# MLP layer 1 and q with the weights as the moving operand in four column groups; w1 in one transfer

## Chip, cores, metric

One core of one Trainium2 chip. The metric is the device time of one execution in microseconds (us), the median of several; all times are of the fast state unless said otherwise. The profile of a kernel is one execution, read as its page, its chain of waits, its timeline, and the records of its DMA packets. PE is the tensor engine (PEld its weight loads), DVE the vector engine, ACT the scalar engine, POOL is GpSimd, and SP issues the big loads.

## The reference

One token, D = 576. Attention over the last 4096 of 32768 cached positions (32 query heads, 16 key heads of 128), an MLP of width 4608, and a gate that mixes the two:

```python
x = A_x
g = _sigmoid((x * gate_w).sum(-1, keepdims=True))
# attention: q = x @ wq; scores over the last W = 4096 keys; softmax; p @ v; then @ wo
a = _A_ref(x, A_k_cache, A_v_cache, A_wq, A_wo)
# MLP: gelu(x @ w1 + b1) @ w2 + b2
b = _B_ref(x, B_w1, B_b1, B_w2, B_b2)
return g * a + (1 - g) * b
```

All operands are bfloat16. The data that must be read are 16.8 MB of keys, as much of values, and 20 MB of weights: 53.6 MB for one token.

## The kernel before

The small rows go through the ACT queue, everything big through the SP queue, in the order in which it is needed. `w1_t` and `wq_t` share their buffers ("B", "A") with later k tiles, so the third k tile (g = 2) can be asked for only when layer 1 is done with w1, and the fourth when q is done with wq.

```python
    rows = kt_pool.tile([2, 8192], BF16, name="rows", tag="kt")
    x_row = rows[0:1, 0:D]
    gw_row = rows[0:1, D : 2 * D]
    b2_row = rows[0:1, 2 * D : 3 * D]
    b1_t = rows[0:2, 3 * D : 3 * D + FH]
    xdup = rows[0:1, 3 * D + FH : 5 * D + FH]
    junk_row = rows[0:1, 5 * D + FH : 6 * D + FH]
    nc.scalar.dma_start(out=x_row, in_=A_x.rearrange("a b d -> (a b) d"))
    nc.scalar.dma_start(out=gw_row, in_=gate_w.rearrange("(o n) -> o n", o=1))
    nc.scalar.dma_start(out=b2_row, in_=B_b2.rearrange("(o n) -> o n", o=1))
    nc.scalar.dma_start(out=b1_t, in_=B_b1.rearrange("(h n) -> h n", h=2))


    w1_t = big.tile([P, NI, FH], BF16, name="w1_t", tag="B")
    w1_src = B_w1.rearrange("d (h n) -> (d h) n", h=2).rearrange("(p i) n -> p i n", i=NI)
    for i0, i1 in ((0, 4), (4, NI)):
        nc.sync.dma_start(out=w1_t[:, i0:i1, :], in_=w1_src[:, i0:i1, :])
    wq_t = big.tile([P, NI, QH], BF16, name="wq_t", tag="A")
    wq_src = A_wq.rearrange("d (h n) -> (d h) n", h=2).rearrange("(p i) n -> p i n", i=NI)
    for i0, i1 in ((0, NI),):
        nc.sync.dma_start(out=wq_t[:, i0:i1, :], in_=wq_src[:, i0:i1, :])
# ... (masks and constants on GpSimd cut)
```

Layer 1 and q use the weights as the stationary operand (`lhsT`), 128 columns at a time, and stream two columns of x through them. That gives each result its place on 128 partitions at once, for 162 + 144 weight loads:

```python
    h_ps = ps_m.tile([P, NF], FP32, name="h_ps", tag="m")
    for j in range(NJ):
        nc.tensor.matmul(
            h_ps[:, j:NF:NJ],
            lhsT=b1_t[:, j:FH:NJ],
            rhs=ident[0:2, 0:2],
            start=(j == 0),
            stop=False,
            skip_group_check=True,
        )
    QZ = 24
    qz_flat = const.tile([P, QZ + 4 * NG * P + 96], BF16, name="qz_flat")
    nc.gpsimd.memset(qz_flat[:].bitcast(FP32), 0.0)
    for i in range(NI):
        for j in range(NJ):
            nc.tensor.matmul(
                h_ps[:, j:NF:NJ],
                lhsT=w1_t[:, i, j:FH:NJ],
                rhs=x2[:, i, :],
                start=False,
                stop=(i == NI - 1 and j == NJ - 1),
                skip_group_check=True,
            )
    hacc = const.tile([P, NF], FP32, name="hacc")
    nc.vector.tensor_copy(out=hacc[:], in_=h_ps[:])
# ... (gelu on DVE and ACT cut)
    q_ps = ps_m.tile([P, Hq], FP32, name="q_ps", tag="m")
    for i in range(NI):
        for j in range(Hq // 2):
            nc.tensor.matmul(
                q_ps[:, j : Hq : Hq // 2],
                lhsT=wq_t[:, i, j * Dh : (j + 1) * Dh],
                rhs=x2[:, i, :],
                start=(i == 0 and j == 0),
                stop=(i == NI - 1 and j == Hq // 2 - 1),
                skip_group_check=True,
            )
    q_b = const.tile([P, Hq], BF16, name="q_b")
    nc.scalar.copy(out=q_b[:], in_=q_ps[:])
# ... (q is spread into qz_flat by four products and four ACT casts)
```

The loads of the caches, by tag, and the transpose that frees them:

```python
    def load(name, tag, cache, g):
        tile_ = big.tile([P, NCK, Dh], BF16, name=name, tag=tag)
        src = cache[0, HB * g : HB * g + HB, Sk - W : Sk, :].rearrange(
            "b (k c) d -> k b (c d)", k=NKP
        )
        nc.sync.dma_start(out=tile_[:].rearrange("p c d -> p (c d)"), in_=src)
        return tile_

    k_t, s_ps, kt = [None] * NG, [None] * NG, {}

    def transpose(g, f):
        if f == 0:
            k_t[g] = load("k_t", "CDBA"[g], A_k_cache, g)
        kt[g, f] = kt_pool.tile([P, SL * Dh], BF16, name="kt", tag="kt")
        keys = k_t[g][:, f * SL : (f + 1) * SL, :]
        queue(
            "dve",
            lambda: nc.vector.transpose(
                out=kt[g, f][:].bitcast(FP32),
                in_=keys.rearrange("p c d -> p (c d)").bitcast(FP32),
            ),
        )
```

The rest (scores, softmax, values, output projection and layer 2, summed in `y_ps`) is the same in both kernels. After the k tiles the order of the loads is two v tiles, w2's first half, the third v tile, a few tail rows of wo (on four of the 16 DMA engines), the fourth v tile, wo in two transfers, and w2's second half in three; the last 16 products follow the last of these.

Of the kernel before, what the change touches and what calls it, by code (L numbers as in the profile page):

```python
# [9 lines left out]
FP32 = mybir.dt.float32  # L10
BF16 = mybir.dt.bfloat16
I32 = mybir.dt.int32
ACT = mybir.ActivationFunctionType
ALU = mybir.AluOpType
# [4 lines left out]
def kernel(  # L19
# [15 lines left out]
    nc = tc.nc  # L35

    P = 128
    D = 576
    Hq, Hkv, Dh = 32, 16, 128
# [7 lines left out]
    FH = F // 2  # L47
    NJ = FH // P
    NF = 2 * NJ
    NI = 2 * D // P  # L50
    QH = Hq * Dh // 2
    DH = D // 2
# [153 lines left out]
    const = ctx.enter_context(tc.tile_pool(name="const", bufs=1))  # L206
    big = ctx.enter_context(tc.tile_pool(name="big", bufs=1, side="right"))
    kt_pool = ctx.enter_context(tc.tile_pool(name="kt_pool", bufs=2, side="right"))
    ps_s = ctx.enter_context(tc.tile_pool(name="ps_s", bufs=2, space=bass.MemoryType.PSUM))
    ps_y = ctx.enter_context(tc.tile_pool(name="ps_y", bufs=1, space=bass.MemoryType.PSUM))  # L210
    ps_m = ctx.enter_context(tc.tile_pool(name="ps_m", bufs=2, space=bass.MemoryType.PSUM))


    rows = kt_pool.tile([2, 8192], BF16, name="rows", tag="kt")
    x_row = rows[0:1, 0:D]
    gw_row = rows[0:1, D : 2 * D]
    b2_row = rows[0:1, 2 * D : 3 * D]
    b1_t = rows[0:2, 3 * D : 3 * D + FH]
    xdup = rows[0:1, 3 * D + FH : 5 * D + FH]
    junk_row = rows[0:1, 5 * D + FH : 6 * D + FH]  # L220
# [5 lines left out]

    w1_t = big.tile([P, NI, FH], BF16, name="w1_t", tag="B")
    w1_src = B_w1.rearrange("d (h n) -> (d h) n", h=2).rearrange("(p i) n -> p i n", i=NI)
    for i0, i1 in ((0, 4), (4, NI)):
        nc.sync.dma_start(out=w1_t[:, i0:i1, :], in_=w1_src[:, i0:i1, :])  # L230
    wq_t = big.tile([P, NI, QH], BF16, name="wq_t", tag="A")
    wq_src = A_wq.rearrange("d (h n) -> (d h) n", h=2).rearrange("(p i) n -> p i n", i=NI)
# [10 lines left out]
    for base, pattern, keep in (  # L243
# [13 lines left out]
        out=is0[:], in0=low[:], scalar1=0.0, scalar2=None, op0=ALU.is_equal  # L257
    )
    alt = is0[:, 0 : 2 * NI].rearrange("p (i t) -> p i t", t=2)
    ones = const.tile([P, P], FP32, name="ones")  # L260
    nc.gpsimd.memset(ones[:], 1.0)
    ident = const.tile([P, P], BF16, name="ident")
    make_identity(nc, ident[:])
    RW = 31
    NZ = 512 + 5 * RW + 1 + 64
    zeros = const.tile([P, NZ + 4 * D], BF16, name="zeros")
    nc.gpsimd.memset(zeros[:].bitcast(FP32), 0.0)
    perm = zeros[:, 0:512].rearrange("p (j b l) -> p j b l", j=4, b=4)
    at31 = zeros[:, 512 : 512 + 5 * RW].rearrange("p (a r) -> p a r", a=5)
# [3 lines left out]
        out=perm,  # L273
        in_=perm,
        pattern=[[-64, 2], [-1, 2], [0, 4], [-2, 32]],
        compare_op=ALU.not_equal,
        fill=1.0,
        base=0,
        channel_multiplier=1,
    )  # L280
    nc.gpsimd.affine_select(
        out=at31,
        in_=at31,
        pattern=[[-RW, 5], [-1, RW]],
        compare_op=ALU.not_equal,
        fill=1.0,
        base=0,
        channel_multiplier=1,
# [3 lines left out]
        out=hi5[:],  # L292
        in_=ones[:, 0:5],
        pattern=[[-RW, 5]],
        compare_op=ALU.is_ge,
        fill=0.0,
        base=0,
        channel_multiplier=1,
    )
    nc.gpsimd.affine_select(  # L300
        out=hi5[:],
        in_=hi5[:],
        pattern=[[RW, 5]],
        compare_op=ALU.is_ge,
        fill=0.0,
        base=RW - 1,
        channel_multiplier=-1,
# [4 lines left out]
        out=hi16[:], in0=is0[:, c0 : c0 + 16], scalar1=-SCALE, scalar2=None, op0=ALU.mult  # L312
# [5 lines left out]
        out=row_of[:],  # L318
        in_=row_of[:],
        pattern=[[0, 16], [-1, HB], [0, 2]],  # L320
        compare_op=ALU.not_equal,
        fill=1.0,
        base=0,
        channel_multiplier=1,
# [4 lines left out]
        out=foreign[:],  # L329
        in_=foreign[:],  # L330
        pattern=[[0, P], [-1, HB]],
        compare_op=ALU.not_equal,
        fill=0.0,
        base=0,
        channel_multiplier=1,
# [4 lines left out]
        out=xdup.rearrange("p (d t) -> p d t", t=2),  # L340
        in_=x_row.rearrange("p (d o) -> p d o", o=1).to_broadcast([1, D, 2]),
    )
    xs_ps = ps_m.tile([P, NI, 1], FP32, name="xs_ps", tag="m")
    for i in range(NI):
        nc.tensor.matmul(  # L345
            xs_ps[:, i, :],
            lhsT=xdup[:, i : 2 * D : NI],
            rhs=one_b[0:1, 0:1],
            start=(i == 0),
            stop=(i == NI - 1),  # L350
            skip_group_check=True,
        )
    x2 = const.tile([P, NI, 2], BF16, name="x2")
    nc.vector.tensor_tensor(
        out=x2[:], in0=xs_ps[:].to_broadcast([P, NI, 2]), in1=alt, op=ALU.mult
    )


# [2 lines left out]
        out=junk_row,  # L361
        in0=x_row,
        in1=gw_row,
        scale=1.0,
        scalar=0.0,
        op0=ALU.mult,
        op1=ALU.add,
# [9 lines left out]
    omg = const.tile([P, 1], FP32, name="omg")  # L377
    nc.vector.tensor_scalar(
        out=omg[:], in0=g_t[:], scalar1=-1.0, scalar2=1.0, op0=ALU.mult, op1=ALU.add
    )  # L380
    b2g = const.tile([1, D], FP32, name="b2g")
    nc.vector.tensor_scalar(
        out=b2g[:], in0=b2_row, scalar1=omg[0:1, 0:1], scalar2=None, op0=ALU.mult
    )
    gh = const.tile([P, 1, 5], FP32, name="gh")
# [1 line left out]
        out=gh[:, 0, :], in0=hi5[:], scalar1=g_t[:, 0:1], scalar2=None, op0=ALU.mult  # L387
# [18 lines left out]
    y_add(ones[0:1, 0:1], b2g[0:1, :], start=True)  # L406


    h_ps = ps_m.tile([P, NF], FP32, name="h_ps", tag="m")
    for j in range(NJ):  # L410
        nc.tensor.matmul(
            h_ps[:, j:NF:NJ],
            lhsT=b1_t[:, j:FH:NJ],
            rhs=ident[0:2, 0:2],
            start=(j == 0),
            stop=False,
            skip_group_check=True,
        )
    QZ = 24
    qz_flat = const.tile([P, QZ + 4 * NG * P + 96], BF16, name="qz_flat")  # L420
    nc.gpsimd.memset(qz_flat[:].bitcast(FP32), 0.0)
    for i in range(NI):
        for j in range(NJ):
            nc.tensor.matmul(  # L424
                h_ps[:, j:NF:NJ],
                lhsT=w1_t[:, i, j:FH:NJ],
                rhs=x2[:, i, :],
                start=False,
                stop=(i == NI - 1 and j == NJ - 1),
                skip_group_check=True,  # L430
            )
    hacc = const.tile([P, NF], FP32, name="hacc")
    nc.vector.tensor_copy(out=hacc[:], in_=h_ps[:])  # L433
    z2 = const.tile([P, NF], FP32, name="z2")
    nc.vector.tensor_tensor(out=z2[:], in0=hacc[:], in1=hacc[:], op=ALU.mult)
    C0 = 0.7978845608028654
    poly = const.tile([P, NF], FP32, name="poly")
    nc.vector.tensor_scalar(
        out=poly[:],
        in0=z2[:],  # L440
        scalar1=2.0 * C0 * 0.044715,
        scalar2=2.0 * C0,
        op0=ALU.mult,
        op1=ALU.add,
    )
    u_t = const.tile([P, NF], FP32, name="u_t")
    nc.vector.tensor_tensor(out=u_t[:], in0=poly[:], in1=hacc[:], op=ALU.mult)
    e_h = const.tile([P, NF], FP32, name="e_h")
    nc.scalar.activation(out=e_h[:], in_=u_t[:], func=ACT.Exp, scale=-1.0)
    nc.vector.tensor_scalar(out=e_h[:], in0=e_h[:], scalar1=1.0, scalar2=None, op0=ALU.add)  # L450
# [1 line left out]
    nc.vector.reciprocal(out=r_t[:], in_=e_h[:])  # L452
    gt = const.tile([P, NF], BF16, name="gt")
    nc.vector.scalar_tensor_tensor(
        out=gt[:], in0=hacc[:], scalar=omg[:, 0:1], in1=r_t[:], op0=ALU.mult, op1=ALU.mult
    )


    q_ps = ps_m.tile([P, Hq], FP32, name="q_ps", tag="m")
    for i in range(NI):  # L460
        for j in range(Hq // 2):
            nc.tensor.matmul(  # L462
                q_ps[:, j : Hq : Hq // 2],
                lhsT=wq_t[:, i, j * Dh : (j + 1) * Dh],
                rhs=x2[:, i, :],
                start=(i == 0 and j == 0),
                stop=(i == NI - 1 and j == Hq // 2 - 1),
                skip_group_check=True,
            )
    q_b = const.tile([P, Hq], BF16, name="q_b")  # L470
    nc.scalar.copy(out=q_b[:], in_=q_ps[:])
    qj_ps = ps_m.tile([P, 4, NG, 8], FP32, name="qj_ps", tag="m")
    for j in range(4):
        nc.tensor.matmul(
# [293 lines left out]
```

## Time and profile before

| | before |
|---|---|
| time | 131.68 us (131.63 to 131.78) |
| span of the profiled run | 130.1 us |
| load queue, share of 16 engines | 96.5% (125.5 us) |
| layer 1 ends / q ready / first k tile transposed from | 24.2 / 32.7 / 36.7 us |
| last load lands / end | 127.2 / 130.1 us |

The lines behind this table stand in the prediction below. A line of the timeline reads: start, duration, engine, source line, operation, output <- inputs, shapes, count; the bracket tells how long the engine sat idle before it and what ended that. Source lines differ between the kernels (L531 before is L569 after); go by the tiles. Two lines of the timeline of the kernel before are needed later, for the small rows of x and of b1:

```profile
6.09 0.75 DVE L339 COPY rows<-rows 1x1152 bf16<-1x1152 bf16 x1 [6.09 <-DMA rows<-in_A_x_dram]
...
10.49 1.28 PE L411 MATMUL h_ps<-ident,rows 2*128 2x2 bf16 x18 [1.36 <-DMA rows<-in_B_b_dram]
```

### The profile page before, as it was taken

To read this page: it belongs to the slowest core of one execution; us is meant where nothing else is said; L and a number is where in the kernel's file an instruction comes from. 1 tells how busy PE (TensorE), PEld (TensorE's weight loads), DVE (VectorE), ACT (ScalarE), POOL (GpSimd) and SP (SyncE) were. 2 spreads that over 40 slices of the span, in tenths; PEclk is the share of its full clock that TensorE was granted. 3 is DMA by queue.
4 is the path that set the end of the run, shared out by engine and by line. 5 is a ranking of instruction groups with operands and counts; after the bars stand their busy time and mean duration, and the time that the engine had idled before them with its cause. 6 is when DMAs were issued, how large, how long until landed. Compare 5 with 4: busy or idle time off the path is not lost.

```text
span 130.1 us, 2403 instructions
## 1 busy us (share of the span) xinstructions
PE 79.7 (61%) x1148; PEld 45.6 (35%) x1077; DVE 52.3 (40%) x48; ACT 8.3 (6%) x18; POOL 9.2 (7%) x26
## 2 busy tenths in 40 slices
PE   0037999476003998939918994995300830899573
PEld 0037679375000121201211120595300830855441
DVE  0153000400079959999999995614000020010001
ACT  2000000003000000030003003011000000000001
POOL 7039700000000000000000000000000000000000
PEclk9999999999999999999997799985555555559999
DMA  6999999799899999999899899899899899999980
GB/s 232 427 431 432 476 424 476 344 484 448 373 458 453 403 433 463 393 433 484 373 433 484 383 423 484 357 432 505 368 433 489 363 438 415 442 401 427 413 363 33
DMA packets 2508, 53.75 MB, mean 413 GB/s; under 512 B 286, under 2 KB 290, under 8 KB 580
## 3 DMA queue, kind: packets, MB, share of 16 engines
q1 hardware_dynamic: 2490, 53.61, 96.5%
q8 instruction: 8, 0.13, 0.4%
q10 hardware_dynamic: 10, 0.01, 0.0%
HBM read 53.62 MB, written 0.00 MB: 412 GB/s over the span
## 4 chain that ended last, share of the span: by engine, by line
DMA 52%; DVE 24%; PE 14%; issue 6%; SPq 2%
DMA k_t<-in_A_k_cache_dram 27%; DMA w_t<-in_B_w_dram 25%; DVE kt L531 19%; PE s_ps L553 7%; PE o_ps L640 5%; DVE m L569 3%; DVE pt L602 2%; PE y_ps L396 1%; SPq L684 1%; DVE mr L572 1%; SPq L691 0%; DVE out_row L736 0%; SPq L234 0%; SPq L230 0%; PE mt_ps L578 0%
## 5 line engine op out<-in xcount | busy, mean ns | idle before, releaser
L553 PE MATMUL s_ps<-kt,qz_flat 128*128 128x512 bf16 x128 | 32.9, 414 | 17.2 <-DVE kt L531 10.4
L531 DVE STREAM_TRANSPOSE kt<-k_t 128x4096 f32<-128x4096 f32 x8 | 35.3, 4433 | 12.2 <-DMA k_t<-in_A_k_cache_dram 10.5
L640 PE MATMUL o_ps<-pt,v_t 128*128 128x8 bf16 x512 | 14.2, 168 | 16.6 <-DMA v_t<-in_A_v_cache_dram 14.7
L553 PEld LDWEIGHTS <-qz_flat 128*128 128x128 bf16 x64 | 6.9, 107 | 40.6 <-issue 40.4
L640 PEld LDWEIGHTS <-v_t 128*128 128x128 bf16 x512 | 14.0, 102 | 17.3 <-DMA v_t<-in_A_v_cache_dram 14.9
L424 PEld LDWEIGHTS <-w_t 128*128 128x128 bf16 x162 | 10.3, 167 | 1.8 <-issue 1.8
L424 PE MATMUL h_ps<-x,w_t 128*128 128x2 bf16 x162 | 10.5, 202 | 0.0
L590 ACT ACTIVATE p_t<-s_ps,negm 128x1024 bf16<-128x1024 f32 x4 | 4.5, 1114 | 50.9 <-DVE negm L586 50.9
L396 PE MATMUL y_ps<-w_t,gt 128*1 128x288 bf16 x72 | 6.3, 329 | 1.2 <-DMA w_t<-in_B_w_dram 1.2
L670 DVE RECIPROCAL rg<-mt_ps 128x32 f32<-128x32 f32 x1 | 0.4, 358 | 15.6 <-PE mt_ps L665 15.6
L602 DVE STREAM_TRANSPOSE pt<-p_t 128x1024 bf16<-128x1024 bf16 x4 | 4.9, 1225 | 2.7 <-ACT p_t L590 2.7
L462 PE MATMUL q_ps<-x,wq_t 128*128 128x2 bf16 x144 | 4.0, 166 | 2.9 <-DMA wq_t<-in_A_wq_dram 2.9
L569 DVE TENSOR_REDUCE m<-s_ps 128x1 f32<-128x1024 f32 x4 | 4.8, 1196 | 1.1 <-PE s_ps L553 1.1
L396 PE MATMUL y_ps<-wo_t,ov 128*1 128x288 bf16 x62 | 4.3, 285 | 1.4 <-DMA wo_t<-in_A_wo_dram 1.4
L736 DVE CAST out_row<-y_ps 1x288 bf16<-1x288 f32 x1 | 0.4, 445 | 11.6 <-PE y_ps L396 11.6
L433 DVE COPY hacc<-h_ps 128x36 f32<-128x36 f32 x1 | 0.2, 196 | 11.9 <-PE h_ps L424 11.9
L462 PEld LDWEIGHTS <-wq_t 128*128 128x128 bf16 x144 | 3.9, 104 | 3.0 <-DMA wq_t<-in_A_wq_dram 3.0
L345 PE MATMUL xs_ps<-one_b,rows 1*128 1x1 bf16 x9 | 0.7, 196 | 6.9 <-DVE rows L339 6.9
L396 PEld LDWEIGHTS <-gt 128*1 128x1 bf16 x72 | 3.3, 92 | 3.4 <-issue 1.6
L694 DVE TENSOR_TENSOR om<-o_ps,rgh 128x128 bf16<-128x128 f32 x1 | 0.3, 291 | 8.6 <-PE o_ps L640 8.6
L396 PEld LDWEIGHTS <-ov 128*1 128x1 bf16 x62 | 2.6, 83 | 2.8 <-issue 1.9
L339 DVE COPY rows<-rows 1x1152 bf16<-1x1152 bf16 x1 | 0.7, 748 | 6.1 <-DMA rows<-in_A_x_dram 6.1
(72 smaller groups left out, 35.5 us busy)
## 6 DMA issues: line engine op xcount, KB each, us to landing
k_t<-in_A_k_cache_dram SPq DMA_DIRECT2D x4, 4096.0 KB, 32.1
v_t<-in_A_v_cache_dram SPq DMA_DIRECT2D x4, 4096.0 KB, 22.8
wq_t<-in_A_wq_dram SPq DMA_DIRECT2D x1, 4608.0 KB, 25.8
w_t<-in_B_w_dram SPq DMA_DIRECT2D x1, 2880.0 KB, 14.1
w_t<-in_B_w_dram SPq DMA_DIRECT2D x1, 2592.0 KB, 22.9
w_t<-in_B_w_dram SPq DMA_DIRECT2D x1, 2304.0 KB, 8.1
wo_t<-in_A_wo_dram SPq DMA_DIRECT2D x1, 2304.0 KB
wo_t<-in_A_wo_dram SPq DMA_DIRECT2D x1, 2160.0 KB
```

Of the source, the lines that this page charges most:

```text
L339: nc.vector.tensor_copy(out=xdup.rearrange("p (d t) -> p d t", t=2), in_=x_row.rearrange("p (d o) -> p d o", o=1).to_broadcast([1, D, 2]),)
L396: last = nc.tensor.matmul(y_out[s], lhsT=vec, rhs=row[:, s * DH : (s + 1) * DH], start=start, stop=stop, skip_group_check=True,)
L424: nc.tensor.matmul(h_ps[:, j:NF:NJ], lhsT=w1_t[:, i, j:FH:NJ], rhs=x2[:, i, :], start=False, stop=(i == NI - 1 and j == NJ - 1), skip_grou ...
L462: nc.tensor.matmul(q_ps[:, j : Hq : Hq // 2], lhsT=wq_t[:, i, j * Dh : (j + 1) * Dh], rhs=x2[:, i, :], start=(i == 0 and j == 0), stop=(i ...
L531: lambda: nc.vector.transpose(out=kt[g, f][:].bitcast(FP32), in_=keys.rearrange("p c d -> p (c d)").bitcast(FP32),),
L553: last = nc.tensor.matmul(s_ps[g][:, u * 512 : (u + 1) * 512].rearrange("p (c k) -> p c k", k=32), lhsT=qz(g, j, 2 * f + half), rhs=kv[:, ...
L569: queue("dve", lambda: nc.vector.reduce_max(out=m1[:], in_=s_ps[g][:], axis=AX.X))
L572: lambda: nc.vector.tensor_scalar(out=mr[:], in0=hi16[:], scalar1=m1[:, 0:1], scalar2=None, op0=ALU.mult),
L590: nc.scalar.activation(out=p_t[:].rearrange("p c k -> p (c k)"), in_=s_ps[g][:], func=ACT.Exp, bias=negm[:, 0:1], scale=SCALE, accum_out=s ...
L602: lambda: nc.vector.transpose(out=pt[:, g, :, :].rearrange("p c q -> p (c q)"), in_=p_t[:].rearrange("p c k -> p (c k)"),),
L640: last = nc.tensor.matmul(o_ps[:, 8 * g : 8 * g + 8, 0], lhsT=v_t[g][:, c, :], rhs=pt[:, g, c % 32, 8 * (c // 32) : 8 * (c // 32) + 8], st ...
L684: nc.sync.dma_start(out=wo_t[:, r0:r1, :].rearrange("p r n -> p (r n)"), in_=wo_src[:, 0 : 4 * RW, :].rearrange("h (a r) n -> h a (r n)", ...
```

## The change

The intent is to take work off the tensor engine: x becomes the stationary operand (padded with zeros to 32 columns), the weights stream through in rows of 288 or 512, and four groups of 32 array columns work on four quarters of the row. 162 + 144 weight loads become 36 + 36 short ones. The price is that the results lie along rows: an ACT copy and a DVE transpose (layer 1), or a copy and four small products (q) put them back. Besides, w1 comes in one transfer, b2's row gets a tile of its own, and b2g (b2 times 1 - g) moves from DVE to GpSimd.

```diff
@@ -214,7 +214,7 @@
     rows = kt_pool.tile([2, 8192], BF16, name="rows", tag="kt")
     x_row = rows[0:1, 0:D]
     gw_row = rows[0:1, D : 2 * D]
-    b2_row = rows[0:1, 2 * D : 3 * D]
+    b2_row = const.tile([1, D], BF16, name="b2_row")[:]
     b1_t = rows[0:2, 3 * D : 3 * D + FH]
     xdup = rows[0:1, 3 * D + FH : 5 * D + FH]
     junk_row = rows[0:1, 5 * D + FH : 6 * D + FH]
@@ -226,7 +226,7 @@
 
     w1_t = big.tile([P, NI, FH], BF16, name="w1_t", tag="B")
     w1_src = B_w1.rearrange("d (h n) -> (d h) n", h=2).rearrange("(p i) n -> p i n", i=NI)
-    for i0, i1 in ((0, 4), (4, NI)):
+    for i0, i1 in ((0, NI),):
         nc.sync.dma_start(out=w1_t[:, i0:i1, :], in_=w1_src[:, i0:i1, :])
     wq_t = big.tile([P, NI, QH], BF16, name="wq_t", tag="A")
     wq_src = A_wq.rearrange("d (h n) -> (d h) n", h=2).rearrange("(p i) n -> p i n", i=NI)
@@ -263,7 +263,8 @@
     make_identity(nc, ident[:])
     RW = 31
     NZ = 512 + 5 * RW + 1 + 64
-    zeros = const.tile([P, NZ + 4 * D], BF16, name="zeros")
+    XZ = NZ + 4 * D
+    zeros = const.tile([P, XZ + 32 * NI + 8], BF16, name="zeros")
     nc.gpsimd.memset(zeros[:].bitcast(FP32), 0.0)
     perm = zeros[:, 0:512].rearrange("p (j b l) -> p j b l", j=4, b=4)
     at31 = zeros[:, 512 : 512 + 5 * RW].rearrange("p (a r) -> p a r", a=5)
@@ -278,6 +279,17 @@
         base=0,
         channel_multiplier=1,
     )
+    x2 = zeros[:, XZ : XZ + 32 * NI].rearrange("p (i m) -> p i m", i=NI)
+    row_is = zeros[:, XZ + 32 * NI : XZ + 32 * NI + 8]
+    nc.gpsimd.affine_select(
+        out=row_is,
+        in_=row_is,
+        pattern=[[-1, 2], [-32, 4]],
+        compare_op=ALU.not_equal,
+        fill=1.0,
+        base=0,
+        channel_multiplier=1,
+    )
     nc.gpsimd.affine_select(
         out=at31,
         in_=at31,
@@ -350,9 +362,8 @@
             stop=(i == NI - 1),
             skip_group_check=True,
         )
-    x2 = const.tile([P, NI, 2], BF16, name="x2")
     nc.vector.tensor_tensor(
-        out=x2[:], in0=xs_ps[:].to_broadcast([P, NI, 2]), in1=alt, op=ALU.mult
+        out=x2[:, :, 0:2], in0=xs_ps[:].to_broadcast([P, NI, 2]), in1=alt, op=ALU.mult
     )
 
 
@@ -379,7 +390,7 @@
         out=omg[:], in0=g_t[:], scalar1=-1.0, scalar2=1.0, op0=ALU.mult, op1=ALU.add
     )
     b2g = const.tile([1, D], FP32, name="b2g")
-    nc.vector.tensor_scalar(
+    nc.gpsimd.tensor_scalar(
         out=b2g[:], in0=b2_row, scalar1=omg[0:1, 0:1], scalar2=None, op0=ALU.mult
     )
     gh = const.tile([P, 1, 5], FP32, name="gh")
@@ -406,33 +417,48 @@
     y_add(ones[0:1, 0:1], b2g[0:1, :], start=True)
 
 
-    h_ps = ps_m.tile([P, NF], FP32, name="h_ps", tag="m")
-    for j in range(NJ):
-        nc.tensor.matmul(
-            h_ps[:, j:NF:NJ],
-            lhsT=b1_t[:, j:FH:NJ],
-            rhs=ident[0:2, 0:2],
-            start=(j == 0),
-            stop=False,
-            skip_group_check=True,
-        )
+    GW = FH // 4
+    h_ps = ps_s.tile([P, 1024], FP32, name="h_ps", tag="s")
+
+    def h_add(g, vec, row, start=False, stop=False):
+        for a in range(2):
+            at = g * GW + a * DH
+            nc.tensor.matmul(
+                h_ps[32 * g : 32 * g + 32, 512 * a : 512 * a + DH],
+                lhsT=vec,
+                rhs=row[:, at : at + DH],
+                start=start,
+                stop=stop,
+                skip_group_check=True,
+            )
+
+    for g in range(4):
+        h_add(g, ident[0:2, 0:32], b1_t, start=True)
     QZ = 24
     qz_flat = const.tile([P, QZ + 4 * NG * P + 96], BF16, name="qz_flat")
     nc.gpsimd.memset(qz_flat[:].bitcast(FP32), 0.0)
     for i in range(NI):
-        for j in range(NJ):
-            nc.tensor.matmul(
-                h_ps[:, j:NF:NJ],
-                lhsT=w1_t[:, i, j:FH:NJ],
-                rhs=x2[:, i, :],
-                start=False,
-                stop=(i == NI - 1 and j == NJ - 1),
-                skip_group_check=True,
-            )
-    hacc = const.tile([P, NF], FP32, name="hacc")
-    nc.vector.tensor_copy(out=hacc[:], in_=h_ps[:])
+        for g in range(4):
+            h_add(g, x2[:, i, :], w1_t[:, i, :], stop=(i == NI - 1))
+    early = kt_pool.tile([P, 4096], FP32, name="early", tag="kt")
+    h_sb = early[:, 0 : 32 * NJ].rearrange("p (j m) -> p j m", m=32)
+    h_t = early[:, 32 * NJ : 64 * NJ].rearrange("p (j m) -> p j m", m=32)
+    nc.scalar.copy(
+        out=h_sb.rearrange("p j (a m) -> p j a m", a=2),
+        in_=h_ps[:].rearrange("p (a w) -> p a w", a=2)[:, :, 0:DH].rearrange(
+            "p a (m j) -> p j a m", j=NJ
+        ),
+    )
+    nc.vector.transpose(
+        out=early[:, 32 * NJ : 64 * NJ], in_=early[:, 0 : 32 * NJ]
+    )
+    hacc = h_t[:, :, 0:2].rearrange("p j h -> p h j")
+
+    def halves(tile_):
+        return tile_[:].rearrange("p (h j) -> p h j", h=2)
+
     z2 = const.tile([P, NF], FP32, name="z2")
-    nc.vector.tensor_tensor(out=z2[:], in0=hacc[:], in1=hacc[:], op=ALU.mult)
+    nc.vector.tensor_tensor(out=halves(z2), in0=hacc, in1=hacc, op=ALU.mult)
     C0 = 0.7978845608028654
     poly = const.tile([P, NF], FP32, name="poly")
     nc.vector.tensor_scalar(
@@ -444,7 +470,7 @@
         op1=ALU.add,
     )
     u_t = const.tile([P, NF], FP32, name="u_t")
-    nc.vector.tensor_tensor(out=u_t[:], in0=poly[:], in1=hacc[:], op=ALU.mult)
+    nc.vector.tensor_tensor(out=halves(u_t), in0=halves(poly), in1=hacc, op=ALU.mult)
     e_h = const.tile([P, NF], FP32, name="e_h")
     nc.scalar.activation(out=e_h[:], in_=u_t[:], func=ACT.Exp, scale=-1.0)
     nc.vector.tensor_scalar(out=e_h[:], in0=e_h[:], scalar1=1.0, scalar2=None, op0=ALU.add)
@@ -452,23 +478,35 @@
     nc.vector.reciprocal(out=r_t[:], in_=e_h[:])
     gt = const.tile([P, NF], BF16, name="gt")
     nc.vector.scalar_tensor_tensor(
-        out=gt[:], in0=hacc[:], scalar=omg[:, 0:1], in1=r_t[:], op0=ALU.mult, op1=ALU.mult
-    )
-
-
-    q_ps = ps_m.tile([P, Hq], FP32, name="q_ps", tag="m")
+        out=halves(gt), in0=hacc, scalar=omg[:, 0:1], in1=halves(r_t), op0=ALU.mult, op1=ALU.mult
+    )
+
+
+    q_ps = ps_s.tile([P, 1024], FP32, name="q_ps", tag="s")
     for i in range(NI):
-        for j in range(Hq // 2):
+        for g in range(4):
             nc.tensor.matmul(
-                q_ps[:, j : Hq : Hq // 2],
-                lhsT=wq_t[:, i, j * Dh : (j + 1) * Dh],
-                rhs=x2[:, i, :],
-                start=(i == 0 and j == 0),
-                stop=(i == NI - 1 and j == Hq // 2 - 1),
+                q_ps[32 * g : 32 * g + 32, 0:512],
+                lhsT=x2[:, i, :],
+                rhs=wq_t[:, i, 512 * g : 512 * (g + 1)],
+                start=(i == 0),
+                stop=(i == NI - 1),
                 skip_group_check=True,
             )
+    q_rows = early[:, 64 * NJ : 64 * NJ + 256].bitcast(BF16)
+    nc.scalar.copy(out=q_rows, in_=q_ps[:, 0:512])
+    qt_ps = ps_m.tile([P, Hq], FP32, name="qt_ps", tag="m")
+    for r in range(4):
+        nc.tensor.matmul(
+            qt_ps[:, r:Hq:4],
+            lhsT=q_rows[:, r * Dh : (r + 1) * Dh],
+            rhs=row_is,
+            start=(r == 0),
+            stop=(r == 3),
+            skip_group_check=True,
+        )
     q_b = const.tile([P, Hq], BF16, name="q_b")
-    nc.scalar.copy(out=q_b[:], in_=q_ps[:])
+    nc.scalar.copy(out=q_b[:], in_=qt_ps[:])
     qj_ps = ps_m.tile([P, 4, NG, 8], FP32, name="qj_ps", tag="m")
     for j in range(4):
         nc.tensor.matmul(
```

## The prediction

> **What bounds the kernel now.** I read the page first, then the chain that ended last in order of time, then the waits of the DMA queue itself, then the timeline of the first 33 us, where the whole change lies. From the page (span; PE by slices; DMA share and GB/s by slices; the DMA queues; HBM bytes; the chain by engine):
>
> ```profile
> span 130.1 us, 2403 instructions
> ...
> DMA  6999999799899999999899899899899899999980
> GB/s 232 427 431 432 476 424 476 344 484 448 373 458 453 403 433 463 393 433 484 373 433 484 383 423 484 357 432 505 368 433 489 363 438 415 442 401 427 413 363 33
> ...
> q1 hardware_dynamic: 2490, 53.61, 96.5%
> q8 instruction: 8, 0.13, 0.4%
> ...
> HBM read 53.62 MB, written 0.00 MB: 412 GB/s over the span
> ## 4 chain that ended last, share of the span: by engine, by line
> DMA 52%; DVE 24%; PE 14%; issue 6%; SPq 2%
> ```
>
> The load queue alone fills 96.5% of 16 engines for 130.1 us, 125.5 us. The DMA row never leaves 7 to 9 between the first slice and the last but one; a slice of 344 or 357 GB/s is followed by one of 484 or 432, so these are packets counted where they end, not holes. The kernel is a 53.6 MB read with arithmetic hidden beneath it. The chain, however, gives DVE 24% and PE 14%. Its pieces in order of time show why this misleads:
>
> ```profile
> 1.65 35.02 DMA k_t<-in_A_k_cache_dram
> ...
> 36.69 4.46 DVE kt L531
> ...
> 94.29 32.93 DMA w_t<-in_B_w_dram
> 127.22 0.04 issue
> 127.27 1.19 PE y_ps L396 x16
> 128.45 0.43 DVE out_row L736
> ```
>
> The middle of that chain (transposes, score products) only leads back to the moment at which the last weights could be issued, 94.29. They then waited 32.9 us in the queue behind other data, so issuing them earlier gains nothing. Whether an issue ever comes late is told by bytes issued less bytes landed, at about 0.43 MB per us from 1.6 us on. At 24.2 us, when the third k tile is issued, 18.4 MB (w1 5.3, wq 4.7, two k tiles of 4.2) have been asked for and about 9.7 landed: 8.7 MB, 20 us of work, lie queued. The third v tile, issued at 79.9 us after 37.8 MB had been asked for and some 33.7 had landed, finds the least: about 4 MB, 10 us. Nothing that waits on arithmetic reaches that far. So the end is: about 0.9 us until the first packet, 126.4 us of streaming, then 2.8 us (the last 16 products, two casts, the store).
>
> The part that changes, from the timeline:
>
> ```profile
> 11.70 3.58 PE L424 MATMUL h_ps<-x,w_t 128*128 128x2 bf16 x55
> ...
> 15.21 1.12 PE L396 MATMUL y_ps<-b2g,ones 1*1 1x288 f32 x4
> ...
> 18.38 5.75 PE L424 MATMUL h_ps<-x,w_t 128*128 128x2 bf16 x90
> 24.16 0.20 DVE L433 COPY hacc<-h_ps 128x36 f32<-128x36 f32 x1 [11.91 <-PE h_ps L424]
> ...
> 27.00 4.00 PE L462 MATMUL q_ps<-x,wq_t 128*128 128x2 bf16 x144 [2.87 <-DMA wq_t<-in_A_wq_dram]
> ...
> 36.69 8.77 DVE L531 STREAM_TRANSPOSE kt<-k_t 128x4096 f32<-128x4096 f32 x2 [10.47 <-DMA k_t<-in_A_k_cache_dram]
> ```
>
> Layer 1 is PE-bound (64 ns a product) and ends at 24.1; q starts when wq lands; q's tail ends at 32.7 (four small ACT casts); and DVE, the next consumer, sits idle 10.5 us until the first k tile lands at 36.67. All that the change speeds up ends before a load that cannot come sooner.
>
> **What the Trainium skill says.** (1) "DMA: Bandwidth & Descriptors", section Bandwidth, "Where 436 GB/s comes from": the ports allow 435.2 GB/s. The trace agrees: its packet records give a median of 1214 ns for 32768 bytes, 27.0 GB/s per engine, 432 for sixteen. The stream is at its ceiling. (2) The same page, "Issuing engines are not separate DMA queues": all queues run on the same 16 engines. So only fewer or cheaper bytes could help. (3) "TensorEngine Tiling (Array Packing)", Performance Considerations: with 32 columns of weights four column tiles run side by side, up to 4 times. The output products, which alternate between two column groups, take 2.61 us for 40 late in the trace, 65 ns each, where a single one is listed with 286 ns; that fits overlap, but no run yet shows four groups. (4) "Runtime: NRT & Kernel Launch", Instruction fetch mechanics: instructions come in 16 KiB blocks of 256 by DMA. The trace agrees: 8 packets of 16384 bytes, each holding its engine 0.98 to 1.10 us.
>
> **The change, part by part.**
>
> Layer 1: removed are 18 bias and 162 weight products of 2 columns (1.28 + 10.5 us busy); in come 8 bias and 72 weight products of 288 columns, with x as weights. Sixteen score products of 512 columns take 3.63 us late in their stage (227 ns each) but 0.43 us each at first, so one of 288 columns takes 128 ns or 240; PE is probably slow here (two of 512 took 1.03 us at 17.4 us, against 0.60 at 50.5). The two of one group share weights and follow each other; the next group can start beside the second. That makes 60 to 125 ns each (half a product's time): 72 of them are 4.3 to 9.0 us. They start late, because w1 now has to land whole (about 14 us instead of the first 4/9 at about 8) and because in PE's order the b2 products come first, which now wait for GpSimd: b2g there follows the last mask (ends at 14.5 before, plus about 0.3 for a new mask), and at the 1.5 to 3.8 ns an element of GpSimd's rows (0.74 us for 512, 0.62 us for 162) takes 0.8 to 2.2 us. So PE starts at 16.7 to 18.2 and ends at 21 to 27, against 24.1.
>
> After it: an ACT copy of 576 columns (0.63 us by the 1114 ns for 1024), a transpose of 576 (0.62 us by the 4433 for 4096), then the same short chain as now. gt is first read at 114.6 us. Free.
>
> q: 144 products (4.0 us) become 36 of 512 columns in four groups, 9 rounds at 227 to 430 ns, 2.0 to 3.9 us. Added are a copy of 512 columns (0.56 us), four small products (0.3 us) and a wait on each side. q's tail ends at 32 to 34 instead of 32.7; the first score product needs the first transposed tile at 41.1. Seven us of slack.
>
> Issue: the third k tile goes out at 21 to 27, with 7 MB or more queued; the fourth at 29 to 32, with about 10. Nothing changes in the stream.
>
> DMA: 128 packets fewer (256 of 18 and 23 KB become 128 of 41 KB), 8 per engine. The medians by size (93 ns for 2304 bytes, 1364 for 36864) give 36.8 ns per KB and 8 ns fixed: 8 x 8 ns plus one 9 ns completion write, 0.07 us per engine. PE loses 488 of its instructions, some two fetch blocks. Linking packets end to start, I sort them into 16 engines: they end over 1.9 us, the last having two fetches; but eight others end within 0.25 us of it, one of them without any fetch. Two fewer are thus worth at most 0.05 us, not 2.
>
> Sum: 0.07 + 0.03 gained on the path, 0 from 5 us of PE: 131.68 - 0.1 = 131.6.
>
> **The rivals.** A, the PE saving shows: if the k tiles' issue mattered, the 3 us that layer 1 might finish earlier would come off, 128.7. For it speaks the queue's wait of 9.2 us for the layer 1 products, the chain's DVE and PE shares, and nothing else; against it, 20 us of queued loads at that moment. B, a new wait takes over: x's small row loads queue behind 41 KB packets (1.5 us each), b2g on GpSimd holds PE, and q's two copies lengthen the path; if these added 8 us and more before 41 us, the transposes would slide and the time would rise by the excess. But 30 us of slack lie further on, since the loads of v and w2 have 10 us or more queued: a slide of 2 to 3 us would still not show. C, engine balance: fetches fall on other engines, and if one meets an engine that carries the extra wo tail rows (8 x 4608 bytes, 1.4 us), the end moves by up to 1.0 us, 132.6. In reverse, a luckier spread gives perhaps 0.3 us, 131.3. I choose "nothing on the path", with C as the spread.
>
> **Range and chances.** The runs of before lie within 0.15 us. 131.6, with 131.0 to 132.3 for eight in ten: C on either side plus the chip's scatter. Faster by over 2% needs 2.6 us, which the stream at 432 of 435 GB/s has not got: 2%. Slower by 2.6 us needs a starved queue: 2%. Within 2%: 96%.
>
> **What would show it right or wrong.** In the changed profile the load queue should still fill about 125.4 us of 16 engines, with about 2346 packets (2490 less 128 and 16) and one or two fetches fewer; DVE's wait for the first k tile should still be about 10 us, ending within 0.3 us of 36.7; PE's busy time falls by 3 us or more with no effect on the span; the last load lands within 0.5 us of 127.2, and 2.8 us follow. If the slices show a hole below 6 in the DMA row, if the first transpose starts over 0.5 us off, or if the queue's share times the span moves by over 0.5 us, the step that failed is the one about the stream.

## The result

131.76 us (131.62 to 132.15, 4 runs) against 131.68: ratio 1.0011, 95% interval 0.9989 to 1.0032, the same. Ratios here are the mean time of one kernel's fast runs over that of the other's fast runs of the same rounds, so not quite the ratio of the quoted medians. The prediction was 131.6, within 2%.

From the page of the changed kernel (span, DMA share by slices, load and instruction queues):

```profile
span 130.4 us, 1959 instructions
...
DMA  7999899899999999999999999999999999999980
...
q1 hardware_dynamic: 2346, 53.61, 96.4%
q8 instruction: 7, 0.11, 0.3%
```

The row of DMA is as full as before, 96.4% of 130.4 us is 125.7 us, and PE's busy time went from 79.7 to 72.9 us without a trace in the span. The chain that ended last, pieces in order of time (start, duration, what):

```profile
1.18 35.65 DMA k_t<-in_A_k_cache_dram
...
95.47 31.98 DMA w_t<-in_B_w_dram
...
127.49 1.19 PE y_ps L407 x16
128.68 0.43 DVE out_row L774
```

It begins and ends as before: the first k tile lands 0.2 us later, the last weights too, and the same tail follows. The timeline of the part that changed:

```profile
7.17 0.75 DVE L351 COPY rows<-rows 1x1152 bf16<-1x1152 bf16 x1 [7.17 <-DMA rows<-in_A_x_dram]
...
15.30 0.67 PE L426 MATMUL h_ps<-rows,ident 2*32 2x288 bf16 x8 [3.57 <-DMA rows<-in_B_b_dram]
...
17.08 1.72 POOL L393 TENSOR_SCALAR b2g<-b_row,omg 1x576 f32<-1x576 bf16 x1
...
18.85 1.12 PE L407 MATMUL y_ps<-b2g,ones 1*1 1x288 f32 x4 [2.88 <-POOL b2g L393]
...
19.90 4.51 PE L426 MATMUL h_ps<-w_t,zeros 128*32 128x288 bf16 x72
...
24.47 0.64 ACT L446 COPY early<-h_ps 128x576 f32<-128x576 f32 x1 [12.54 <-PE h_ps L426]
...
26.04 3.67 PE L488 MATMUL q_ps<-wq_t,zeros 128*32 128x512 bf16 x36 [1.62 <-DMA wq_t<-in_A_wq_dram]
...
36.95 4.45 DVE L569 STREAM_TRANSPOSE kt<-k_t 128x4096 f32<-128x4096 f32 x1 [9.09 <-DMA k_t<-in_A_k_cache_dram]
```

The 72 products of layer 1 take 4.51 us, 63 ns each, where 162 took 10.5. Yet layer 1 ends at 24.5 us, no earlier than before, because it starts only at 19.9. Three things are new in front of it: the bias row comes at 15.3 us instead of 10.5, w1 has to land whole (near 15 us), and b2g is made on GpSimd. The one that ends last is b2g: PE waits for it until 18.85, and in PE's order the b2 products stand before the layer. So the saving in this stage was eaten by new waits. But in the last line DVE still idles 9.09 us until the first k tile lands; whether any of the saving could have reached the end is what the experiments below test.

### The profile page after: what moved, and what is told of

Its sections match the earlier page's. It is cut to its first block, busy times and chain, and to the rows that moved or that the text cites. A ratio compares the mean times of both kernels' runs of the same rounds, so it can differ in the third digit from the quotient of the medians.

```text
span 130.4 us, 1959 instructions
## 1 busy us (share of the span) xinstructions
PE 72.9 (56%) x944; PEld 33.5 (26%) x833; DVE 52.3 (40%) x47; ACT 9.5 (7%) x20; POOL 11.0 (8%) x28
## 3 DMA queue, kind: packets, MB, share of 16 engines
q1 hardware_dynamic: 2346, 53.61, 96.4%
## 4 chain that ended last, share of the span: by engine, by line
DMA 52%; DVE 24%; PE 14%; issue 7%; SPq 2%; DVEq 0%
DMA k_t<-in_A_k_cache_dram 27%; DMA w_t<-in_B_w_dram 25%; DVE kt L569 19%; PE s_ps L591 7%; PE o_ps L678 5%; DVE m L607 3%; DVE pt L640 2%; PE y_ps L407 1%; SPq L722 1%; DVE mr L610 1%; SPq L729 0%; DVE out_row L774 0%; SPq L234 0%; PE mt_ps L616 0%; DVE negm L624 0%
## 5 line engine op out<-in xcount | busy, mean ns | idle before, releaser
L708 DVE RECIPROCAL rg<-mt_ps 128x32 f32<-128x32 f32 x1 | 0.4, 357 | 15.3 <-PE mt_ps L703 15.3
L452 DVE STREAM_TRANSPOSE early<-early 128x576 f32<-128x576 f32 x1 | 0.8, 778 | 10.3 <-ACT early L446 10.3
L488 PE MATMUL q_ps<-wq_t,zeros 128*32 128x512 bf16 x36 | 3.7, 586 | 1.6 <-DMA wq_t<-in_A_wq_dram 1.6
L426 PE MATMUL h_ps<-w_t,zeros 128*32 128x288 bf16 x72 | 4.5, 445 | 0.0
L407 PE MATMUL y_ps<-b2g,ones 1*1 1x288 f32 x4 | 1.1, 657 | 2.9 <-POOL b2g L393 2.9
L357 PEld LDWEIGHTS <-rows 1*128 1x128 bf16 x9 | 0.6, 152 | 8.0 <-DVE rows L351 8.0
```

Of the source, the lines that this page charges most:

```text
L357: nc.tensor.matmul(xs_ps[:, i, :], lhsT=xdup[:, i : 2 * D : NI], rhs=one_b[0:1, 0:1], start=(i == 0), stop=(i == NI - 1), skip_group_check ...
L407: last = nc.tensor.matmul(y_out[s], lhsT=vec, rhs=row[:, s * DH : (s + 1) * DH], start=start, stop=stop, skip_group_check=True,)
L426: nc.tensor.matmul(h_ps[32 * g : 32 * g + 32, 512 * a : 512 * a + DH], lhsT=vec, rhs=row[:, at : at + DH], start=start, stop=stop, skip_gr ...
L488: nc.tensor.matmul(q_ps[32 * g : 32 * g + 32, 0:512], lhsT=x2[:, i, :], rhs=wq_t[:, i, 512 * g : 512 * (g + 1)], start=(i == 0), stop=(i = ...
```

## The experiments

The theory (called the stream theory): the end is set by the last byte of a load queue that never runs dry; anything that layer 1 and q do before the queue would run dry is free. Rival A: their time is on the path, and it was the new waits that cancelled the gain. Rival B: a new wait took the place of the old. A third, C of the prediction, is the balance of the 16 DMA engines. Ten kernels ran, in three sessions; each is compared with the kernel before on the same chip (131.60, 131.63 and 131.51 us there; the 131.68 of the table is from the measurement of the change). Two of them, small_pk and w2_less, change the loads and stand outside the table.

| kernel | layer 1 ends, us | time, us | ratio to before (95%) |
|---|---|---|---|
| groups, w1 in two, b2g on DVE (early) | 16.7 | 131.53 | 0.9996 (0.9984 to 1.0008) |
| groups, w1 in two (w1_two) | 20.7 | 131.73 | 1.0003 (0.9990 to 1.0016) |
| before | 24.2 | 131.68 | 1 |
| the change | 24.5 | 131.76 | 1.0011 (0.9989 to 1.0032) |
| before, w1 in one (w1_one) | 28.5 | 131.76 | 1.0012 (1.0000 to 1.0024) |
| the change + 2 passes of zeros (pad2) | 28.6 | 131.97 | 1.0024 (0.9984 to 1.0063) |
| + 4 passes (pad4) | 32.3 | 131.81 | 1.0007 (0.9982 to 1.0032) |
| + 6 passes (pad6) | 38.1 | 132.89 | 1.0122 (1.0063 to 1.0180) |
| + 10 passes (pad10) | 47.9 | 137.20 | 1.0429 (1.0409 to 1.0449) |
| + 14 passes (pad14) | 56.7 | 145.88 | 1.1113 (1.1076 to 1.1149) |

"Layer 1 ends" is the start of the copy out of `h_ps` in the timeline of the profiled run. The time of pad14 is the median of its three fast runs; with the slow one it is 146.21.

### The column groups alone (w1_two)

```diff
-    for i0, i1 in ((0, NI),):
+    for i0, i1 in ((0, 4), (4, NI)):
         nc.sync.dma_start(out=w1_t[:, i0:i1, :], in_=w1_src[:, i0:i1, :])
```

> The column groups alone: the changed kernel with w1 in two transfers again. Stream theory (the end is the last byte of a load queue that never runs dry): 131.7 us, within 0.3 of both kernels; the row of x lands near 6.1 us again instead of 7.2, and the bias rows near 10.5 instead of 15.3, because the small loads then wait for one 18 or 23 KB packet each instead of one of 41 KB. Rival A (the arithmetic of the first 36 us is on the path): a change of 1 us or more, since layer 1 could start earlier.

131.73 us (5 runs). As the stream theory says. The bias row came back to its old time, by the timeline:

```profile
10.71 0.67 PE L426 MATMUL h_ps<-rows,ident 2*32 2x288 bf16 x8 [1.36 <-DMA rows<-in_B_b_dram]
```

So it is the single transfer that delays the small rows. The packet records show how. The rows of x, gate, b2 and b1 on the other queue move one at a time between packets of w1. In the changed kernel the second part of b1 begins 9.3 us after the row of x, and the small rows and their completion writes between the two follow each other in steps of 1.4 to 1.6 us, the time of a packet of 41472 bytes (median 1533 ns). In the kernel before it begins 3.9 us after the row of x, in steps of 0.3 to 1.0 us, between packets of 18 and 23 KB (687 and 855 ns). A small load beside a large one waits a whole packet of it at every turn.

### The single transfer alone (w1_one)

The same two lines exchanged the other way, in the kernel before.

> The single transfer alone: the kernel before, with w1 in one transfer and the old 162 products. Stream theory: 131.7 us within 0.3, although layer 1 now ends near 29.5 us instead of 24.2 (bias rows at 15.3, then 1.3 of bias, 10.5 of products, 1.1 for b2, about 1.5 of gaps) and q's tail near 35.5 instead of 32.7; the first score product still starts near 41. Rival A: the 5 us by which layer 1 ends later come out at the end, 136 to 137.

131.76 us (5 runs). From its timeline:

```profile
18.28 10.20 PE L424 MATMUL h_ps<-x,w_t 128*128 128x2 bf16 x162
28.52 0.20 DVE L433 COPY hacc<-h_ps 128x36 f32<-128x36 f32 x1 [13.81 <-PE h_ps L424]
...
36.97 8.77 DVE L531 STREAM_TRANSPOSE kt<-k_t 128x4096 f32<-128x4096 f32 x2 [6.40 <-DMA k_t<-in_A_k_cache_dram]
```

Layer 1 ends 4.4 us later than before, and the first transpose starts 0.3 us later, with 6.4 us of idle time still in front of it. Rival A wanted 136 to 137 us.

### The column groups without what held them up (early)

```diff
-    for i0, i1 in ((0, NI),):
+    for i0, i1 in ((0, 4), (4, NI)):
         nc.sync.dma_start(out=w1_t[:, i0:i1, :], in_=w1_src[:, i0:i1, :])
...
-    nc.gpsimd.tensor_scalar(
+    nc.vector.tensor_scalar(
         out=b2g[:], in0=b2_row, scalar1=omg[0:1, 0:1], scalar2=None, op0=ALU.mult
```

> The column groups without what held them up: w1 in two transfers and b2g on the vector engine again. Layer 1 should end near 17.5 us, some 6.5 earlier than in either kernel. Stream theory: 131.7 us within 0.3. Rival A: those 6.5 us come off, 125 to 126; even a tenth of it would be 131.0.

131.53 us (5 runs), ratio 0.9996. Timeline:

```profile
12.77 3.88 PE L426 MATMUL h_ps<-w_t,zeros 128*32 128x288 bf16 x70
...
16.71 0.64 ACT L446 COPY early<-h_ps 128x576 f32<-128x576 f32 x1 [7.34 <-PE h_ps L426]
...
36.71 8.77 DVE L569 STREAM_TRANSPOSE kt<-k_t 128x4096 f32<-128x4096 f32 x2 [16.62 <-DMA k_t<-in_A_k_cache_dram]
```

Here the intent of the change is fully reached: layer 1 ends at 16.7 us, 7.5 us earlier than before. The table splits what held it up in the changed kernel: w1 in two transfers brings its end from 24.5 to 20.7 us, b2g back on DVE from there to 16.7. Of the 7.5 us, 6.2 turn into idle time of DVE (16.62 us where the kernel before has 10.47), and the rest goes into the new copy and transpose; DVE's first transpose of keys starts at 36.71, where it started before (36.69). Rival A is refuted from this side too, and rival B with it: with the new waits gone, nothing is gained either.

### The packet's own cost (small_pk)

```diff
-    w1_t = big.tile([P, NI, FH], BF16, name="w1_t", tag="B")
+    w1_p = big.tile([P, NI, FH + 32], BF16, name="w1_t", tag="B")
+    w1_t = w1_p[:, :, 0:FH]
```

> The packet's own cost: the changed kernel, w1 still in one transfer, but into rows padded by 64 bytes so that a row moves in nine packets of 4608 bytes rather than one of 41472: 1024 packets more, 64 per engine. With the 8 ns per packet fitted in the prediction: 0.5 us more stream; less up to 0.3 because the first packet of each engine, which took 0.78 us longer than the later ones of 41 KB, is small: 131.8 to 132.3. Rival: a packet costs 20 ns or more, 133 and above. The bias rows should land before 8 us.

132.67 us (6 runs), ratio 1.0084, above the upper end of what was expected. The first k tile comes later:

```profile
37.58 8.77 DVE L570 STREAM_TRANSPOSE kt<-k_t 128x4096 f32<-128x4096 f32 x2 [13.49 <-DMA k_t<-in_A_k_cache_dram]
```

That is 0.63 us later than in the changed kernel. The packet records split it, with the store of the result as a common mark (its packet less its issue). The first packet starts 0.41 us later than in the changed kernel; then 0.34 us more pass from the run's first packet to the engines' first packets of wq, in their mean (13581 against 13237 ns). Nine packets of 178 ns replace one of 1533, 69 ns more for eight packets more: 8.6 ns a packet, as fitted. What I had not thought of is the start, later by 0.41 us with nine times as many packets in the one transfer. The saving at the first packet did not come either: it is spread over the first small ones (0.71 us above 178 ns each in the first six or so, against 0.78 us for the first big one). As expected, the bias rows had landed by 6.9 us: beside packets of 178 ns a turn comes sooner. The two parts make 0.75 us, and the last packet of the run ends 0.76 us later. So what is added to the stream or to its start is paid at the end, unlike the 7.5 us on PE.

### Zeros to lengthen layer 1 (pad2, pad4, pad6, pad10, pad14)

```diff
-            h_add(g, x2[:, i, :], w1_t[:, i, :], stop=(i == NI - 1))
+            h_add(g, x2[:, i, :], w1_t[:, i, :])
+    for r in range(6):  # 2, 4, 6, 10 or 14
+        for i in range(NI):
+            for g in range(4):
+                h_add(g, om_t[:, 0:32], w1_t[:, i, :], stop=(r == 5 and i == NI - 1))
```

`om_t` holds zeros at that time, so nothing is added to the sum and the result stays correct.

> Dose 1: the changed kernel with two further passes over w1 whose weights are zero (they add nothing), 144 products at 62 ns, 9 us more of layer 1, which ends near 33.4 us; q near 37, its tail near 40, still before the first transposed tile at 41.4. Stream theory: 131.7 us within 0.3. Rival A (arithmetic on the path): 9 us more, 140.7. Rival B (a new wait of 8 us takes over): just at its edge, up to 1 us more.

> Dose 2: four passes of zeros, layer 1 ends near 42.4 us; the third k tile is issued then, when the queue holds some 2 us; q's tail ends near 49, so the scores start some 7.5 us late and the third v tile is issued at 87 to 88, with 1.5 us in the queue. Stream theory: 131.7 to 132.7 us. Rival A: 18 us more, 149.7. Rival B: the 7.5 us by which the scores are late, 139.

> Dose 3: six passes of zeros, layer 1 ends near 51.4 us. The queue (18.4 MB asked for, about 0.43 MB per us) is empty near 44.3, so it stands still until the third k tile is issued, plus about 1.5 us to its first packets: a hole of 8 to 9 us in the DMA row. Stream theory: 139.5 to 141 us, by that hole alone. Rival A: 27 us more, 158.7. Rival B: the 16 us by which the scores are late, 148.

131.97, 131.81 and 132.89 us. The doses were smaller than planned (layer 1 ended at 28.6, 32.3 and 38.1 us instead of 33.4, 42.4 and 51.4), because the passes of zeros took about half the time of the first 72 products. The cause lies in the clock and not in the zeros: 16 products start per us at first and 32 later, and the pace changes at the first clock record of the trace, which grants the full clock (23.8 us in pad6; 25.3 in pad14, where the zeros that began before it still run at the slow pace). So pad4 shows only that 8 us more of layer 1 cost nothing (DVE still waits for the first k tile):

```profile
32.30 0.64 ACT L452 COPY early<-h_ps 128x576 f32<-128x576 f32 x1 [20.68 <-PE h_ps L426]
...
37.03 8.77 DVE L575 STREAM_TRANSPOSE kt<-k_t 128x4096 f32<-128x4096 f32 x2 [1.35 <-DMA k_t<-in_A_k_cache_dram]
```

And pad6, with 13.6 us more, costs 1.3 us over the kernel before although its DMA row has no hole. The packet records of pad6 show where the extra time lies. I sorted the packets into 16 engines by linking each packet's end to the next one's start, requiring of every engine the same sequence of sizes. The ends of the engines' last packets (us from the first packet of the run):

```
             no extras            one extra                last engine
before       124.6 to 125.1 (4)   125.9 to 126.4 (11)      126.47, one fetch
the change   124.8 to 125.2 (6)   126.0 to 126.6 (9)       126.78, its data at 125.9, then a fetch
pad6         124.6 to 125.4 (4)   125.9 to 126.6 (11)      127.67, two fetches
```

An extra is one fetch of a 16 KB instruction block (about 1.0 us) or the eight packets of wo's tail (1.4 us). Only pad6's last engine has two fetches amid its data, and it ends 1.09 us after the next, about one fetch. Its page has more fetches because of the added products:

```profile
q8 instruction: 9, 0.15, 0.4%
```

This is the mechanism of rival C. It rests on one trace and on the linking; no run moved a fetch by itself. All four runs of pad6 lie 1.1 us or more above the kernel before (132.72 to 134.18); only the fastest was profiled, so whether the others met two fetches too is not known, and one fetch would not explain 134.18.

Then two bigger doses, with expectations corrected for the faster pace:

> The doses so far fell short, since the passes of zeros ran at 26 to 40 ns a product, so two bigger ones. Ten passes: layer 1 ends near 47 us (38.0 with six, 2.3 us a pass). The queue is empty near 44.3, so it stands still for 3 to 4 us until the third k tile's first packets come (47 plus 0.8 us); later issues follow with some reserve left. Stream theory: 134.7 to 136 us, by the hole, plus up to 1.1 us if one DMA engine again meets two instruction fetches. Rival A (arithmetic on the path): 23 us more, 154.5. Rival B (the 11 us by which the first transposes are late): 143.

> Fourteen passes: layer 1 ends near 56 us, a hole of 12 to 13 us in the DMA row from 44.3 on. Stream theory: 143.5 to 146 us, and the difference to ten passes is the difference of the two layer 1 ends, one for one, now that the reserve is used up. Rival A: 32 us more, 163.5. Rival B: 20 us more, 152.

137.20 and 145.88 us (one of pad14's four runs was in the slow state and is left out). Busy time by stretches (window: length, then busy time and count for PE, PEld, DVE, ACT, POOL; granted clock, DMA share, GB/s), of the changed kernel, of pad10 and of pad14:

```profile
44.00:48.00 4.00, 4.00 (x15) 0.79 (x7) 2.25 (x2) 0.00 (x0) 0.00 (x0) 0.72 1.01 434
```

```profile
44.00:48.00 4.00, 3.63 (x109) 2.04 (x58) 0.00 (x0) 0.15 (x1) 0.00 (x0) 1.00 0.12 47
48.00:52.00 4.00, 2.80 (x43) 1.56 (x31) 1.40 (x4) 1.92 (x6) 0.00 (x0) 1.00 0.71 258
```

```profile
44.00:48.00 4.00, 4.00 (x140) 2.00 (x64) 0.00 (x0) 0.00 (x0) 0.00 (x0) 1.00 0.17 66
48.00:52.00 4.00, 4.00 (x140) 2.06 (x68) 0.00 (x0) 0.00 (x0) 0.00 (x0) 1.00 0.01 4
52.00:56.00 4.00, 4.00 (x140) 2.07 (x68) 0.00 (x0) 0.00 (x0) 0.00 (x0) 1.00 0.02 4
```

Here is the hole: most engines have nothing from between 44 and 45 us on, because the third k tile waits for layer 1 to give up w1's buffer. (In these two runs tail rows of wo, 0.07 and 0.15 MB, were also issued ahead of that tile, which the edit did not ask for; it is too little to matter here.) The emptying comes where the sum of bytes in the expectation put it (44.3). From ten to fourteen passes layer 1 ends 8.9 us later and the kernel 8.7 us later: past the edge, one for one within the scatter. Extended back, the line meets 131.7 us at 47.9 - 5.5 = 42.4 us. Before that, from 16.7 to 32.3 us, the end moves by at most 0.44 us, without order. Pad14 came within what was expected, pad10 1.2 us above it (0.1 with the 1.1 us allowed for fetches). The restart of the empty queue was dearer than the 0.8 us I allowed: by the packet records the first packet of the third k tile starts 1.36 us after the issue in both runs, and the engines' first packets of it take 1.55 us (pad10) and 1.65 us (pad14) in the mean, where 1.21 is usual. No run varied the restart by itself.

### Fewer bytes (w2_less; a wrong result on purpose)

```diff
-    nc.sync.dma_start(out=w2_t[:, 0:NJ, :], in_=w2_src[:, 0])
+    nc.sync.dma_start(out=w2_t[:, 0:8, :], in_=w2_src[:, 0, 0:8])
...
-            y_add(gt[:, f : f + 1], w2_t[:, f, :])
+            y_add(gt[:, f : f + 1], w2_t[:, f % 8, :])
...
-    late = [(gt, f, w2_t[:, f, :]) for f in range(6, NJ)]
+    late = [(gt, f, w2_t[:, f % 8, :]) for f in range(6, NJ)]
```

> Fewer bytes late in the queue: the changed kernel loads 8 instead of 18 of the rows of each partition in w2's first half and uses them again for the rest (a wrong result on purpose). 1.47 MB less at 0.43 MB per us. Stream theory: 3.4 us less, 128.3 us. Rival (the chain through the transposes and score products sets the end): no change, 131.7.

128.36 us, ratio 0.9748 (0.9723 to 0.9773). The result is wrong, as meant. Its page and its chain:

```profile
q1 hardware_dynamic: 2346, 52.14, 96.4%
```

```profile
94.34 29.65 DMA w_t<-in_B_w_dram
123.99 0.04 issue
124.04 1.19 PE y_ps L407 x16
```

The issue of the last weights is at 94.3 us as in the kernel before (95.5 in the changed kernel, whose edit this is), but they land 3.2 us earlier than there: the queue in front of them is shorter. The share of 96.4% stays. 2.7% of the bytes are worth 2.5% of the time; the arithmetic, with as many products as before, allows it.

## Why the prediction was right

**The bound.** The stream was named as the bound, with the chain's DVE and PE shares as misleading. Shown: bytes count (w2_less, 3.3 us for 1.47 MB, 3.4 expected), 7.5 us less of layer 1 do not (early), nor do 4 or 8 us more (w1_one, pad4). Rival A is refuted by these, and rival B by early and pad14 (152 by B, 143.5 to 146 by the stream, 145.9 measured).

**The reserve.** "20 us of work, lie queued" when layer 1 gives up its buffer: by the doses, layer 1 could end at about 42.4 us instead of 24.2, 18.2 us later, before the time follows one for one. The 20 us left out what it takes to start again (1.36 us to the first packet, and slower first packets). The 42.4 is a line through two doses, carried on below them; no run lies between 38.1 and 47.9.

**Part by part.** Layer 1's products were put at 4.3 to 9.0 us and took 4.51; b2g at 0.8 to 2.2 and took 1.72; q's at 2.0 to 3.9 and took 3.67; DVE's wait was to end within 0.3 us of 36.7 and ended at 36.95; the packets were 2346 to the number. Missed: PE was to start the layer between 16.7 and 18.2 us and started at 19.9. I had listed "small row loads queue behind 41 KB packets" under rival B, but not put it into the sum; the gate's row was used 2.6 us later (10.27 against 7.67) and held back everything on GpSimd, up to b2g. Two slips did no harm. PE loses 448 instructions, not 488 (2225 to 1777 on the pages). And 65 ns against a listed 286 was no fair measure of overlap, since a listed duration is longer than the pace (the score products are listed with 377 ns and follow each other every 227): against the 128 ns that the prediction itself reckons for 288 columns, 65 shows two groups side by side.

**The small gain in the stream was not there.** I counted 0.07 us per engine for 128 packets fewer. The packets' own cost was right (8 ns), but the first packet of each engine was slow: 2311 ns in the mean where the second took 1534 (0.78 us more), against 1103 before, where the median packet of that size takes 687 (0.42 us more). From the run's first packet to the engines' first packets of wq (their mean) it is 13165 ns before and 13237 after: 0.07 us lost instead of gained. Nor did two instruction blocks go, but one (8 packets to 7). And my first linking of packets gave the last engine of the kernel before two fetches; with the stricter linking each of its eight fetches fell on an engine of its own. All this is some 0.2 us, less than the runs scatter (131.62 to 132.15), so the 0.08 us between the two medians is not explained and need not be.

**What stays open.** Whether the second fetch is the cause of pad6's 1.1 us was not tested by itself, and where the time starts to rise was not measured more closely. And no version ran that beats the kernel before: the best, 131.53 us, is the same within its interval.

## What to carry to other kernels

Before speeding up a stage that waits for loads on both sides, write down bytes asked for less bytes landed at the moment when the stage releases a buffer: here it said 20 us, and no saving in the stage could show. A chain of waits that runs through compute proves nothing where its last piece is a load that waited 30 us in a full queue. When transfers are merged into bigger rows, look at the small loads beside them: they get a turn once per packet, and at 41 KB a packet the last of five rows was nearly 5 us later.

## What the Trainium skill lacked or had wrong

- "DMA: Bandwidth & Descriptors", Queues, rings and completion order, says that an engine changes between queues at packets, of 9 to 17 descriptors as a rule. It gives no time for it. Here the rows of 1 to 5 KB beside a 41 KB row got one turn in 1.53 us, the time of a single packet record of that row, and b1 was used at 15.3 us instead of 10.5.
- The same page has no figure for how much longer an engine's first packet of a load takes when its queue was idle. At the start of a run it was 0.42 us longer than the usual one at 18 KB and 0.78 us at 41 KB, after a hole in the queue 0.34 and 0.43 us at 32 KB (pad10, pad14).
- Its figure of about 10.5 ns a packet is for transfers issued from GpSimd. For the SP queue these runs show 8 to 9 ns (fit over sizes; small_pk 8.6), and in small_pk a start 0.41 us later for nine times the packets in one transfer.
- "Runtime: NRT & Kernel Launch", Instruction fetch mechanics, calls the cost of a block mostly hidden. Each block of 16 KiB took its DMA engine 0.9 to 1.1 us here, and in a kernel bound by its loads the engine with two of them ended 1.09 us after the others (pad6, one trace).
- "TensorEngine Tiling (Array Packing)", Theoretical Speedup, says up to 4 times for four column tiles and gives no measured case. Here q's 36 products of 512 columns took 2.13 us in w2_less, 59 ns each, where one alone takes 227 ns by the score products: 3.8 times.
- "TensorE: Matmul & The Clock Gate", Part 1, tells of an array that starts at half rate. The runs agree by their pace: the same q took 3.67 us in the changed kernel, 3.80 in early and 2.13 in w2_less. The page also warns that clock events in traces are not reliable. Here they fit the pace, but they begin late, which the page does not mention: the trace of the changed kernel has no clock record before 29.2 us and that of w2_less none before 24.5, and the clock row shows a stretch without a record as 9. So in the ninth slice, where q runs, the row says 9 for both, although only w2_less's q starts after a record of the full clock; early has a record of half the clock there, and its row says 5. Before the first record the clock has to be read from the pace of the products. The clock rows of the changed kernel, of w2_less and of early, and the q of the last two:

```profile
PEclk9999999999555599999997799985555555559999
```

```profile
PEclk9999999999555599999998699995555555556999
```

```profile
PEclk9999995559555589999999998699555555558999
```

```profile
26.21 2.13 PE L488 MATMUL q_ps<-wq_t,zeros 128*32 128x512 bf16 x36 [1.94 <-DMA wq_t<-in_A_wq_dram]
```

```profile
25.84 3.80 PE L488 MATMUL q_ps<-wq_t,zeros 128*32 128x512 bf16 x36 [9.19 <-DMA wq_t<-in_A_wq_dram]
```
